# A transformer block's gates: one row of the modulation contracted on VectorE and GpSimd, the other in half-width matvecs

## The chip, the cores and the metric

The kernel runs on one core of a Trainium2 chip. The metric is the time of one execution on the device in microseconds (us), lower being better. Before the change it is 837.8 us, the median of four runs (836.96 to 838.38).

## What is computed

A block of linear attention followed by a gated feed-forward layer, both modulated by a vector c. With S = 2048 rows, D = 1024 and F = 3584, all in bfloat16:

```python
mod = (silu(c) @ w_mod).reshape(6, D)          # w_mod is 1024 x 6144
sa, ca, ga, sb, cb, gb = mod
h = layernorm(x) * (1 + ca) + sa
x = x + ga * linear_attention(h, wqkv, wo)     # 32 heads; q and k through elu + 1
h = layernorm(x) * (1 + cb) + sb
x = x + gb * ((silu(h @ w_gate) * (h @ w_up)) @ w_down)
```

The change concerns ga and gb, two rows of 1024 values, each a product of silu(c) with a 1024 x 1024 slice of w_mod.

## The kernel before

The rows are worked in four chunks of 512 (`NSC`), each of four tiles of 128 rows. TensorE runs one long sequence, kept in program order by `mm` (L98): for each chunk the k and v projections (`k_phase`, `v_phase`), with the k-v product of the chunk before (`kv_phase`) between; then the q projections, the folding of the k-v matrix into wo, and the attention output `wo_tile` (L561) of the first chunk. Then, for each chunk, `gate_up` (L596) and `down` (L622).

`gate_up` walks seven blocks of 512 hidden columns (index `fb`). For a block it loads 1 MB of gate and 1 MB of up weights, both on the synchronous engine's DMA queue. The block has four pairs of accumulators (`fj`), a gate and an up one, eight matmuls of 512 columns each. ScalarE takes the silu of the gate accumulator (L616); VectorE multiplies it with the up accumulator into `gu` (L617), which frees both. The accumulators come from a pool of four PSUM banks. `down` computes eight pieces of 128 x 512 for a chunk, multiplies each by the broadcast row `gb_bc` (L638), adds the residual `x1r` and stores it. Between the pieces the next chunk's `wo_tile`s run: their statistics on VectorE, `rstd` on GpSimd (L211), the store of x1 on GpSimd's DMA queue (L585), and a DMA transpose into `h2T` on the synchronous queue (L588).

In the first `gate_up` a table of callbacks hangs more work behind the last gu product of some blocks (L618 to L620, called at L667). `late_den` makes three den sums on TensorE after block 0, and then, after blocks 0, 2 and 4, broadcasts the reciprocals of the denominators to `rbc` through GpSimd's DMA queue (`den_spread`); after blocks 2, 4 and 6 it multiplies `pq` by them on VectorE (`den_apply`, L427).

The modulation rows are made in three ways. sa and ca come early, in an opening that is interleaved by hand. sb, cb, ga and gb come from `mod_rows` (L364 on): four column blocks of w_mod, 1 MB each (`wml`, loaded by `mod_load`), are multiplied by silu(c), replicated over 32 columns (`sc32`). Four matmuls stand in the four 32-column groups of TensorE at once, one per column block, so all four rows lie in one PSUM bank, `modr`. ScalarE copies the bank to SBUF (`mrow`), GpSimd's queue stores one row of each group to DRAM (`mrow_scratch`), and `mod_spread` reads them back: for k = 0 broadcast over partitions into `ga_bc` and `gb_bc` (L381), for k = 1 as columns sb and cb. The first call stands in chunk 2's k phase with the columns of ga and gb, the second in chunk 3's with those of sb and cb. `ga_bc` is multiplied into wo (L524).

SBUF tiles come from rotating pools; `k8` has 19 buffers of 8 KB a partition for weights and activations, `k2` holds five `x_sb` and four `xn` tiles of 128 x 1024 in bfloat16, `x1p` three f32 tiles `x1`. A scheduler orders each engine's instructions, except where `mm` or `in_order` pins them and where `issue_after` queues work behind a named instruction.

Of the kernel before, what the change touches and what calls it, by code (L numbers as in the profile page):

```python
# [1 line left out]

# [5 lines left out]

# [1 line left out]
ALU = mybir.AluOpType  # L10
BF16 = mybir.dt.bfloat16
F32 = mybir.dt.float32
# [9 lines left out]
def kernel(  # L22
# [13 lines left out]
    nc = tc.nc  # L36
    P = nc.NUM_PARTITIONS
    _, S, D = A_x.shape
# [4 lines left out]
    DC = D // P  # L43
# [3 lines left out]
    NSC = S // SCW  # L47
    STC = SCW // P
    NB = 512
# [16 lines left out]
    wm_v = w_mod.rearrange("(j p) n -> p j n", p=P)  # L66
    c_v = c.rearrange("o (j p) -> (o j) p", p=P)

    const = ctx.enter_context(tc.tile_pool(name="const", bufs=1))
    dram = ctx.enter_context(tc.tile_pool(name="dram", bufs=1, space=DRAM))  # L70
    k8 = ctx.enter_context(tc.tile_pool(name="k8", bufs=19))
    k2 = ctx.enter_context(tc.tile_pool(name="k2", bufs=5))
    x1p = ctx.enter_context(tc.tile_pool(name="x1p", bufs=3))
    ep = ctx.enter_context(tc.tile_pool(name="ep", bufs=3))
    yp = ctx.enter_context(tc.tile_pool(name="yp", bufs=2))
    small = ctx.enter_context(tc.tile_pool(name="small", bufs=4))
# [20 lines left out]
    def mm(out, lhsT, rhs, start, stop):  # L97
        return tc.keep_in_program_order(nc.tensor.matmul(out, lhsT=lhsT, rhs=rhs, start=start, stop=stop))  # L98
# [4 lines left out]
    def big(name, shape):  # L103
        return k8.tile([P] + shape, BF16, name=name, tag="k8")

    def acc_a():
        return pa.tile([P, NB], F32, name="acc", tag="pa")

    def acc_b(name, shape=(NB,), dt=F32):
        return pb.tile([P] + list(shape), dt, name=name, tag="pb")  # L110
# [65 lines left out]
    nc.gpsimd.memset(base[:, :, 1, :], 1.0)  # L176

    scT = const.tile([P, DC], BF16, name="scT")
    sc32 = const.tile([P, DC, 32], BF16, name="sc32")

    sca = const.tile([P, 2, DC], F32, name="sca")
# [4 lines left out]
    sbT = const.tile([P, DC], F32, name="sbT")  # L186
    cb1T = const.tile([P, DC], F32, name="cb1T")
    ga_t = ep.tile([P, NB], F32, name="e")
    ga_bc = ga_t[:].bitcast(BF16)
    gb_bc = const.tile([P, D], BF16, name="gb_bc")  # L190
# [9 lines left out]
    def build_masks():  # L200
        nc.gpsimd.memset(zmask[:], 0.0)
        for h in range(HPC):
            rs = slice(h * DH, (h + 1) * DH)
            for hg in range(HG):
                nc.gpsimd.memset(zmask[rs, hg, HG * h + hg:HG * h + hg + 1], 1.0)
# [52 lines left out]
    def ln1(sc):  # L258
        hTs[sc] = big("hT", [DC, SCW])
        for t in range(STC):  # L260
            ln1_norm(*ln1_stats(sc, t))
# [45 lines left out]
    def k_phase(sc, lo, hi):  # L307
        if lo == 0:
            pks[sc] = big("pk", [STC, D])
        for g in k_groups[lo:hi]:  # L310
            accs = [acc_a()]
            k_mms(sc, [g], accs)
            k_evac(sc, [g], accs)
# [28 lines left out]
    def kv_phase(sc):  # L342
        kvp = acc_b("kvp", (HG, 2, DH))
        for hg in range(HG):
            for t in range(STC):
                for i in range(HPC):
                    mm(kvp[i * DH:(i + 1) * DH, hg, :, :], lhsT=pks[sc][:, t, hg * P + i * DH:hg * P + (i + 1) * DH],
                       rhs=v_ones(vs[sc], t * D + hg * P + i * DH), start=(t == 0), stop=(t == STC - 1))
        kvv = kvp[:].rearrange("p g k e -> p g (k e)")[:, :, 0:DH + 1]
        if sc == 0:  # L350
            nc.vector.tensor_copy(out=kv_acc, in_=kvv)
        else:
            nc.vector.tensor_tensor(out=kv_acc, in0=kv_acc, in1=kvv, op=ALU.add)

    def mod_load(cols):
        blks = []
        for lo in cols:
            t = big("wml", [DC, NB])
            nc.sync.dma_start(out=t[:], in_=wm_v[:, :, lo:lo + NB])
            blks.append(t)  # L360
        return blks

    def mod_rows(blks):
        ps = acc_b("modr")  # L364
        for j in range(DC):
            for g in range(4):
                mm(ps[32 * g:32 * g + 32, :], lhsT=sc32[:, j, :], rhs=blks[g][:, j, :],
                                 start=(j == 0), stop=(j == DC - 1))
        row = small.tile([P, NB], BF16, name="mrow", bufs=1)
        nc.scalar.copy(out=row[:], in_=ps[:])  # L370
        return row

    mrow_dram = dram.tile([2, 4, NB], BF16, name="mrow_scratch")

    def mod_spread(k, row):
        for g in range(4):
            nc.gpsimd.dma_start(out=mrow_dram[k, g:g + 1, :], in_=row[32 * g:32 * g + 1, :])
        if k == 0:
            for dst, g in ((ga_bc, 0), (gb_bc[:], 2)):
                src = mrow_dram[0, g:g + 2, :].rearrange("g n -> (g n)").unsqueeze(0).to_broadcast([P, D])  # L380
                nc.gpsimd.dma_start(out=dst, in_=src)  # L381
        else:
            cols = small.tile([P, 2 * DC], BF16, name="mcol", bufs=1)
            with nc.allow_non_contiguous_dma(reason="2048 elements, once"):
                nc.gpsimd.dma_start(out=cols[:], in_=mrow_dram[1].rearrange("g (i p) -> p (g i)", p=P))
            nc.vector.tensor_copy(out=sbT[:], in_=cols[:, 0:DC])
            nc.vector.tensor_scalar_add(out=cb1T[:], in0=cols[:, DC:2 * DC], scalar1=1.0)

    def modulate_all(hT, scaleT, biasT):
        for cc in range(DC):  # L390
# [51 lines left out]
    with in_order(nc.vector, nc.scalar, nc.gpsimd):  # L442
        mod_ps = acc_b("mod_ps")
        mm(mod_ps[:, A * 64:A * 64 + DC], lhsT=c_sb[:], rhs=ident[0:DC, 0:DC], start=True, stop=True)
        for g in range(4):
            mm(mod_ps[32 * g:32 * g + 32, 0:A * 64], lhsT=ident[:, 0:32], rhs=base_t[:, 0:A * 64],
               start=True, stop=False)
# [39 lines left out]
        k_evac(0, gs8, accs8)  # L487
    with tc.issue_after(last_on[nc.gpsimd.engine]):
        build_masks()

    for sc in range(NSC):
        if sc > 0:
            k_phase(sc, 0, 2)
            kv_phase(sc - 1)
            k_phase(sc, 2, 4)
            if sc >= 2:
                mod_spread(sc - 2, mod_rows(blks))
            k_phase(sc, 4, 8)
            if sc == 1:
                blks = mod_load([2 * D, 2 * D + NB, 5 * D, 5 * D + NB])  # L500
            if sc == 2:
                blks = mod_load([3 * D, 3 * D + NB, 4 * D, 4 * D + NB])
        v_phase(sc)
        if sc + 1 < NSC:
            with tc.issue_after(last_on[nc.vector.engine] if sc == 0 else last_phi[-5].ins):
                ln1(sc + 1)
        if sc == 0:
            q_phase(0, 0, 6)
        if sc + 1 < NSC:
            with tc.issue_after(last_phi[0].ins):  # L510
                modulate_all(hTs[sc + 1], ca1T, saT)
        if sc == 0:
            q_phase(0, 6, 8)
        if sc + 2 < NSC:
            for st in range((sc + 2) * STC, (sc + 3) * STC):
                load_x(st, nc.sync)
        if sc == 2:
            wo = [big("wo", [4, D]) for _ in range(2)]
            for h in range(2):
                for g in range(4):  # L520
                    nc.sync.dma_start(out=wo[h][g * DH:(g + 1) * DH, :, :], in_=wo_v[h, g])
            for cc in range(DC):
                w = wo[cc // 4][:, cc % 4, :]
                nc.vector.tensor_tensor(out=w, in0=w, in1=ga_bc, op=ALU.mult)  # L524
# [5 lines left out]
                            in1=zmask[:], op=ALU.mult)  # L530
# [62 lines left out]
    last_w = {}  # L593
    last_mm = {}

    def gate_up(sc, between=None):  # L596
        guT[sc] = []
        for fb in range(NFB):
            wb = []
            for view in (wg_v, wu_v):  # L600
                w = big("wgu", [DC, FBW])
                last_w[sc] = nc.sync.dma_start(out=w[:], in_=view[:, :, fb * FBW:(fb + 1) * FBW])
                wb.append(w)
            for fj in range(FPB):
                f = fb * FPB + fj
                if f % GPT == 0:
                    guT[sc].append(big("gu", [min(GPT, FC - f), SCW]))
                ps = []
                for w in wb:
                    acc = acc_a()  # L610
                    for cc in range(DC):
                        last_mm[sc] = mm(acc[:], lhsT=w[:, cc, fj * P:(fj + 1) * P], rhs=h2Ts[sc][:, cc, :],
                                              start=(cc == 0), stop=(cc == DC - 1))
                    ps.append(acc)
                sg = ep.tile([P, NB], F32, name="e")
                nc.scalar.activation(out=sg[:], in_=ps[0][:], func=ACT.Silu)  # L616
                gm = nc.vector.tensor_tensor(out=guT[sc][f // GPT][:, f % GPT, :], in0=ps[1][:], in1=sg[:], op=ALU.mult)  # L617
            if between and fb in between:  # L618
                with tc.issue_after(gm.ins):
                    between[fb]()  # L620
# [38 lines left out]
    def late_den(sc, sums=()):  # L659
        for s in sums:  # L660
            den_sum(s)
        if sc > 1:
            den_apply(sc - 1)
        if sc < NSC:
            den_spread(sc)

    gate_up(0, {0: lambda: late_den(1, range(1, NSC)), 2: lambda: late_den(2), 4: lambda: late_den(3),  # L667
                6: lambda: late_den(NSC)})
    wd = []
    for b in range(FC // WDF):  # L670
        w = big("wd", [WDF, D])
# [38 lines left out]
```

## Time and profile before

| | |
|---|---|
| median of four runs | 837.8 us |
| the profiled execution, whole | 836.96 us |
| its span in the profile | 835.1 us |
| busy: VectorE, ScalarE, GpSimd | 308.3, 168.9, 61.4 us |
| read from HBM / written | 108.53 / 12.72 MB |
| first `gate_up` on TensorE | 208.5 to 306.8 us |

The profile records one execution; starts are in us from the beginning of the span. PE is TensorE, PEld its weight loads, DVE VectorE, ACT ScalarE, POOL GpSimd, SP the synchronous engine; L617 is line 617. A row of the timeline gives start, duration, engine, line, operation, the tile written and those read, shapes, the count of merged instructions, and in brackets how long the engine was idle before and what ended it. A matmul's recorded duration spans its whole way through the array, so successive ones overlap; what it costs is the distance to the next start. A DMA row on an engine's queue is its issue; the transfer lands later.

### The profile page before, as it was taken

To read this page: it belongs to the slowest core of one execution; us is meant where nothing else is said; L and a number is where in the kernel's file an instruction comes from. 1 tells how busy PE (TensorE), PEld (TensorE's weight loads), DVE (VectorE), ACT (ScalarE), POOL (GpSimd) and SP (SyncE) were. 2 spreads that over 40 slices of the span, in tenths; PEclk is the share of its full clock that TensorE was granted. 3 is DMA by queue.
4 is the path that set the end of the run, shared out by engine and by line. 5 is a ranking of instruction groups with operands and counts; after the bars stand their busy time and mean duration, and the time that the engine had idled before them with its cause. 6 is when DMAs were issued, how large, how long until landed. Compare 5 with 4: busy or idle time off the path is not lost.

```text
span 835.1 us, 11163 instructions
## 1 busy us (share of the span) xinstructions
PE 823.7 (99%) x4560; PEld 378.6 (45%) x4641; DVE 308.3 (37%) x598; ACT 168.9 (20%) x253; POOL 61.4 (7%) x167
## 2 busy tenths in 40 slices
PE   8999999999999999999999999999999999999998
PEld 3444444444444444444444444444444444444444
DVE  5755643587413325521122344211114431111122
ACT  3445443334211111101111110111110101111000
POOL 2101201111130001100000010000001100000000
PEclk9999999999999999999999999999999999999999
DMA  9793790129987447336434182662504529610011
GB/s 331 287 291 79 243 210 1 30 66 273 364 200 260 151 151 208 120 114 219 146 109 144 44 228 95 224 217 77 175 1 152 164 70 345 225 53 1 18 58 51
DMA packets 126755, 129.33 MB, mean 155 GB/s; under 512 B 34032, under 2 KB 108272, under 8 KB 126192
## 3 DMA queue, kind: packets, MB, share of 16 engines
q1 hardware_dynamic: 122368, 114.97, 44.8%
q0 software_dynamic: 4048, 13.25, 5.3%
q8 instruction: 36, 0.59, 0.3%
q10 hardware_dynamic: 288, 0.40, 0.1%
q14 instruction: 15, 0.12, 0.0%
HBM read 108.53 MB, written 12.72 MB: 145 GB/s over the span
## 4 chain that ended last, share of the span: by engine, by line
PE 96%; DMA 2%; issue 1%; DVE 0%; ACT 0%; ACTq 0%; SPq 0%
PE acc L98 88%; PE a_ps L98 7%; DMA wme<-in_w_mod_dram 1%; DMA wml<-in_w_mod_dram 1%; PE modr L98 0%; PE kvp L98 0%; PE den L98 0%; PE mod_ps L98 0%; DVE wo L548 0%; PE wf L98 0%; DVE pq L291 0%; ACT eb L288 0%; ACTq L125 0%; PE tp L101 0%; SPq L134 0%
## 5 line engine op out<-in xcount | busy, mean ns | idle before, releaser
L98 PE MATMUL acc<-h2T,wgu 128*128 128x512 bf16 x1756 | 385.7, 379 | 1.9
L98 PEld LDWEIGHTS <-wgu 128*128 128x128 bf16 x1792 | 175.3, 98 | 211.3
L98 PE MATMUL acc<-wd,gu 128*128 128x512 bf16 (+2 forms) x908 | 195.2, 372 | 0.9
L617 DVE TENSOR_TENSOR gu<-acc,e 128x512 bf16<-128x512 f32 x112 | 77.5, 692 | 299.3 <-PE acc L98 288.2
L616 ACT ACTIVATE e<-acc 128x512 f32<-128x512 f32 x112 | 67.0, 598 | 374.6 <-PE acc L98 363.2
L98 PEld LDWEIGHTS <-gu 128*128 128x128 bf16 x924 | 89.3, 98 | 104.5
L98 PEld LDWEIGHTS <-hT 128*128 128x128 bf16 x512 | 49.6, 98 | 60.0 <-issue 0.9
L638 DVE TENSOR_TENSOR e<-acc,gb_bc 128x512 f32<-128x512 f32 (+2 forms) x33 | 22.3, 675 | 132.2 <-PE acc L98 125.9
L98 PE MATMUL acc<-wk,hT 128*128 128x512 bf16 x248 | 56.5, 379 | 0.8 <-issue 0.3
L98 PE MATMUL a_ps<-wo,pq 128*128 128x512 bf16 x250 | 56.9, 379 | 0.3
L98 PE MATMUL acc<-hT,wq 128*128 128x512 bf16 x247 | 55.6, 379 | 0.9 <-issue 0.6
L98 PE MATMUL acc<-wv,hT 128*128 128x512 bf16 x251 | 55.6, 379 | 0.3
L288 ACT ACTIVATE eb<-acc 128x512 bf16<-128x512 f32 x64 | 37.9, 596 | 74.4 <-PE acc L98 71.2
L227 ACT ACTIVATE xn<-x,nmr,rstd 128x1024 bf16<-128x1024 f32 x16 | 19.8, 1240 | 126.3 <-POOL nmr L225 126.3
L585 POOL DMA_DIRECT2D x_scratch<-x x16 | 9.7, 608 | 418.2 <-DVE x L578 418.2
L98 PEld LDWEIGHTS <-pq 128*128 128x128 bf16 x256 | 25.0, 98 | 30.2
L98 PEld LDWEIGHTS <-wq 128*128 128x128 bf16 x256 | 24.6, 98 | 29.8 <-issue 0.9
L289 DVE TENSOR_SCALAR eb<-eb 128x512 bf16<-128x512 bf16 x64 | 18.3, 290 | 49.7 <-ACT eb L288 49.6
L578 DVE TENSOR_TENSOR x<-a_ps,x_sb 128x512 f32<-128x512 f32 x32 | 22.1, 691 | 7.9 <-PE a_ps L98 7.1
L211 POOL TENSOR_TENSOR rstd<-veps,neg_half 128x1 f32<-128x1 f32 x32 | 17.9, 560 | 73.6 <-DVE veps L209 71.3
L326 ACT CAST v<-acc 128x512 bf16<-128x512 f32 x32 | 18.4, 583 | 23.1 <-PE acc L98 22.5
L641 DVE TENSOR_TENSOR ob<-e,x1r 128x512 bf16<-128x512 f32 (+2 forms) x33 | 22.3, 675 | 1.0
(76 smaller groups left out, 259.2 us busy)
## 6 DMA issues: line engine op xcount, KB each, us to landing
wgu<-in_B_w_gate_dram SPq DMA_DIRECT2D x28, 1024.0 KB, 7.0
wgu<-in_B_w_up_dram SPq DMA_DIRECT2D x28, 1024.0 KB, 7.9
x_sb<-in_A_x_dram SPq DMA_DIRECT2D x32, 256.0 KB, 6.5
wml<-in_w_mod_dram SPq DMA_DIRECT2D x8, 1024.0 KB, 9.1
x_scratch<-x POOLq DMA_DIRECT2D x16, 512.0 KB, 3.0
x1r<-x_scratch SPq DMA_DIRECT2D x31, 256.0 KB, 2.8
wd<-in_B_w_down_dram SPq DMA_DIRECT2D x7, 1024.0 KB, 6.1
rbc<-rden_scratch POOLq DMA_DIRECT2D x16, 256.0 KB, 5.5
```

The costliest lines, as they stand in the source:

```text
L98: return tc.keep_in_program_order(nc.tensor.matmul(out, lhsT=lhsT, rhs=rhs, start=start, stop=stop))
L211: nc.gpsimd.tensor_tensor(out=rstd[:, 0:n], in0=veps[:, 0:n], in1=neg_half[:].to_broadcast([P, n]), op=ALU.pow)
L227: nc.scalar.activation(out=dst, in_=src, func=ACT.Identity, bias=nmr[:], scale=rstd[:, 0:1])
L288: nc.scalar.activation(out=e[:], in_=acc, func=ACT.Exp)
L289: nc.vector.tensor_scalar(out=e[:], in0=e[:], scalar1=1.0, scalar2=PHI_EPS, op0=ALU.min, op1=ALU.add)
L326: nc.scalar.copy(out=v[:, t * D + nb * NB:t * D + (nb + 1) * NB], in_=acc[:])
L578: nc.vector.tensor_tensor(out=x1[:, ns], in0=a_ps[:], in1=x_t[:, ns], op=ALU.add)
L585: nc.gpsimd.dma_start(out=x1_dram[st * P:(st + 1) * P, :], in_=x1[:])
L616: nc.scalar.activation(out=sg[:], in_=ps[0][:], func=ACT.Silu)
L617: gm = nc.vector.tensor_tensor(out=guT[sc][f // GPT][:, f % GPT, :], in0=ps[1][:], in1=sg[:], op=ALU.mult)
L638: nc.vector.tensor_tensor(out=yt, in0=y_ps, in1=gb_bc[:, ns], op=ALU.mult)
L641: nc.vector.tensor_tensor(out=ob, in0=yt, in1=x1r, op=ALU.add)
```

## The change

The row gb no longer goes through TensorE. `gb_load` reads the 1024 x 1024 slice of w_mod as eight tiles of 128 x 1024, 256 KB each, into five `x_sb` and three `xn` buffers, on the synchronous queue behind the weight loads of the first gate/up's block 1. `gb_sum` multiplies each by its column of silu(c) (`scf`, an f32 copy) and accumulates in f32 in `gb_acc`: one product and four multiply-adds after block 1, three after block 3. Then one GpSimd instruction sums `gb_acc` over the 128 partitions and leaves the total in every partition of `gb_bc`.

The row ga keeps its matmuls. Its 1024 columns now fill all four 32-column groups with 256 columns each (`ga_rows`), from two `wml` blocks instead of four; row stores and broadcast follow with pieces of 256. `mod_spread` keeps only its branch for sb and cb.

```diff
+    scf = const.tile([P, DC], F32, name="scf")
...
+    def gb_load():
+        for j in range(DC):
+            t = k2.tile([P, D], BF16, name="x_sb") if j < 5 else k2.tile([P, D], BF16, name="xn", bufs=4)
+            nc.sync.dma_start(out=t[:], in_=wm_v[:, j, 5 * D:6 * D])
+            gb_rows.append(t)
+
+    def gb_sum(lo, hi):
+        for j in range(lo, hi):
+            t, sc = gb_rows[j], scf[:, j:j + 1]
+            if j == 0:
+                nc.vector.tensor_scalar(out=gb_acc[:], in0=t[:], scalar1=sc, scalar2=None, op0=ALU.mult)
+            else:
+                nc.vector.scalar_tensor_tensor(out=gb_acc[:], in0=t[:], scalar=sc, in1=gb_acc[:], op0=ALU.mult, op1=ALU.add)
+
+    def ga_rows(blks):
+        ps = acc_b("modr")
+        H2 = NB // 2
+        for j in range(DC):
+            for g in range(4):
+                mm(ps[32 * g:32 * g + 32, 0:H2], lhsT=sc32[:, j, :], rhs=blks[g // 2][:, j, (g % 2) * H2:(g % 2 + 1) * H2],
+                   start=(j == 0), stop=(j == DC - 1))
+        row = small.tile([P, NB], BF16, name="mrow", bufs=1)
+        nc.scalar.copy(out=row[:, 0:H2], in_=ps[:, 0:H2])
+        for g in range(4):
+            nc.gpsimd.dma_start(out=mrow_dram[0, g:g + 1, 0:H2], in_=row[32 * g:32 * g + 1, 0:H2])
+        nc.gpsimd.dma_start(out=ga_bc.rearrange("p (g n) -> p g n", g=4),
+                            in_=mrow_dram[0, :, 0:H2].unsqueeze(0).to_broadcast([P, 4, H2]))
...
-        if k == 0:
-            for dst, g in ((ga_bc, 0), (gb_bc[:], 2)):
-                src = mrow_dram[0, g:g + 2, :].rearrange("g n -> (g n)").unsqueeze(0).to_broadcast([P, D])
-                nc.gpsimd.dma_start(out=dst, in_=src)
...
     with tc.issue_after(last_on[nc.gpsimd.engine]):
         build_masks()
+        nc.gpsimd.tensor_copy(out=scf[:], in_=scT[:])
...
-            if sc >= 2:
-                mod_spread(sc - 2, mod_rows(blks))
+            if sc == 2:
+                ga_rows(blks)
+            if sc == 3:
+                mod_spread(1, mod_rows(blks))
             k_phase(sc, 4, 8)
             if sc == 1:
-                blks = mod_load([2 * D, 2 * D + NB, 5 * D, 5 * D + NB])
+                blks = mod_load([2 * D, 2 * D + NB])
...
-    gate_up(0, {0: lambda: late_den(1, range(1, NSC)), 2: lambda: late_den(2), 4: lambda: late_den(3),
-                6: lambda: late_den(NSC)})
+    def gb_first():
+        with tc.issue_after(last_w[0].ins):
+            gb_load()
+        gb_sum(0, 5)
+
+    def gb_last():
+        gb_sum(5, DC)
+        nc.gpsimd.partition_all_reduce(gb_bc[:], gb_acc[:], P, bass_isa.ReduceOp.add)
+
+    gb_acc = x1p.tile([P, D], F32, name="x1")
+    gate_up(0, {0: lambda: late_den(1, range(1, NSC)), 1: gb_first, 2: lambda: late_den(2), 3: gb_last,
+                4: lambda: late_den(3), 6: lambda: late_den(NSC)})
```

In the instruction streams of the changed kernel, VectorE's order in block 2 is one product and two multiply-adds, a gu product, two multiply-adds, the next gu product; the three of block 3 stand together before the first gu product of block 4. On GpSimd the sum over partitions stands after the first of the last four `rbc` broadcasts and before the other three. One library instruction precedes it, and another stands between the x1 store and `rstd` of the next chunk's first `wo_tile`. The eight row loads stand on the synchronous queue between the weights of block 1 and those of block 2.

More of the change, by code (lines that the diff above doesn't have):

```diff
@@ L4 @@
 import concourse.tile as tile
-from concourse import bass_utils, mybir
+from concourse import bass_isa, bass_utils, mybir
 from concourse._compat import with_exitstack
@@ L353, in kv_phase @@
             nc.vector.tensor_tensor(out=kv_acc, in0=kv_acc, in1=kvv, op=ALU.add)
+    def gb_load():
[23 more added lines that the diff above has]
+                            in_=mrow_dram[0, :, 0:H2].unsqueeze(0).to_broadcast([P, 4, H2]))
+    gb_rows = []
     def mod_load(cols):
@@ L377, in mod_spread @@
             nc.gpsimd.dma_start(out=mrow_dram[k, g:g + 1, :], in_=row[32 * g:32 * g + 1, :])
-        if k == 0:
-            for dst, g in ((ga_bc, 0), (gb_bc[:], 2)):
-                src = mrow_dram[0, g:g + 2, :].rearrange("g n -> (g n)").unsqueeze(0).to_broadcast([P, D])
-                nc.gpsimd.dma_start(out=dst, in_=src)
[L382 to L387, printed above, removed]
+        cols = small.tile([P, 2 * DC], BF16, name="mcol", bufs=1)
+        with nc.allow_non_contiguous_dma(reason="2048 elements, once"):
+            nc.gpsimd.dma_start(out=cols[:], in_=mrow_dram[1].rearrange("g (i p) -> p (g i)", p=P))
+        nc.vector.tensor_copy(out=sbT[:], in_=cols[:, 0:DC])
+        nc.vector.tensor_scalar_add(out=cb1T[:], in0=cols[:, DC:2 * DC], scalar1=1.0)
     def modulate_all(hT, scaleT, biasT):
```

## The prediction

> **What bounds the kernel now.** I read the page from the top: busy times, then the chain that ended last, then the timelines of TensorE, VectorE and GpSimd over the stretches that the change touches. From the page:
>
> ```profile
> PE 823.7 (99%) x4560; PEld 378.6 (45%) x4641; DVE 308.3 (37%) x598; ACT 168.9 (20%) x253; POOL 61.4 (7%) x167
> ...
> PE 96%; DMA 2%; issue 1%; DVE 0%; ACT 0%; ACTq 0%; SPq 0%
> ```
>
> TensorE works for 823.7 of 835.1 us and the chain is 96% TensorE. Time can go only where TensorE's own work shrinks; it can come wherever another engine makes it wait. Of the 11.4 us idle, 3.05 lie in the first 30 us and 4.2 after 600 us, where nothing changes. The clock row is 9 in all 40 slices and the windows give a granted clock of 1.00, so no clock is to be won. TensorE's timeline around the two mod-row blocks, and through the first gate/up stage:
>
> ```profile
> 95.12 1.91 PE L98 MATMUL modr<-wml,sc 128*32 128x512 bf16 x32
> 96.96 7.08 PE L98 MATMUL acc<-wk,hT 128*128 128x512 bf16 x31
> ...
> 208.50 13.98 PE L98 MATMUL acc<-h2T,wgu 128*128 128x512 bf16 x63
> 222.41 1.52 PE L98 MATMUL den<-pq,Zden 128*32 128x128 bf16 x96
> 223.86 83.05 PE L98 MATMUL acc<-h2T,wgu 128*128 128x512 bf16 x376
> 306.75 6.21 PE L98 MATMUL acc<-wd,gu 128*128 128x512 bf16 x27
> ```
>
> The first column is the start. The first mod-row block holds TensorE from 95.12 until the next projection starts at 96.96, 1.84 us. The stage runs without a gap from 208.50 to 306.75: seven blocks of four pairs, a pair 3.455 us (the spacing of VectorE's products below), and 1.45 us of den sums. VectorE and GpSimd in that stage:
>
> ```profile
> 265.59 0.69 DVE L617 TENSOR_TENSOR gu<-acc,e 128x512 bf16<-128x512 f32 x1 [2.76 <-PE acc L98]
> ...
> 279.40 0.69 DVE L617 TENSOR_TENSOR gu<-acc,e 128x512 bf16<-128x512 f32 x1 [2.76 <-PE acc L98]
> 280.01 2.48 DVE L427 TENSOR_TENSOR pq<-pq,rbc 128x1024 bf16<-128x1024 bf16 x4
> 282.85 0.69 DVE L617 TENSOR_TENSOR gu<-acc,e 128x512 bf16<-128x512 f32 x1 [0.36 <-PE acc L98]
> ...
> 241.67 1.94 POOL L419 DMA_DIRECT2D rbc<-rden_scratch  x4 [1.29 <-PE acc L98]
> 317.44 0.57 POOL L585 DMA_DIRECT2D x_scratch<-x  x1 [73.83 <-DVE x L578]
> 318.53 0.56 POOL L211 TENSOR_TENSOR rstd<-veps,neg_half 128x1 f32<-128x1 f32 x1 [0.52 <-DVE veps L209]
> ```
>
> VectorE is idle 2.76 us of each 3.455. GpSimd is idle from 243.6 to 317.4.
>
> **Removed from TensorE.** The first block's 32 matmuls go from 512 to 256 columns. They run four at a time: 1.84 us / 8 groups = 230 ns a group. The den sums have the same shape with 128 columns: 1.45 us / 24 = 60.4 ns. Between the two a column costs (230 − 60.4)/384 = 0.44 ns, so a 256-column group is 60.4 + 128 × 0.44 = 117 ns, eight are 0.94 us, and **0.90 us** goes. The 0.16 us that the next projection waited for a wml load at 91.7 may go too; I don't count it. The second block stays 1.84.
>
> **Early transfers.** Two 1 MB wml loads leave the synchronous queue at 49 to 56 us, and the gate's broadcast leaves GpSimd's (0.56 us of issue at 103.0). The ga broadcast now moves pieces of 256 elements. Nothing waits for less than it did: the wo product that reads ga waited for TensorE (3.1 us), not for it. The scheduler reorders some statistics and normalisations at 97 to 107 us; the hT tile made there is modulated by 115.0 and used at 117.69. Those 2.7 us hide a slip; a larger one would be TensorE's.
>
> **The eight row loads, 2 MB.** They stand on the synchronous queue behind the second block's weights (issued 199.74 and 200.98), ahead of the third's. From 217 to 231 us the DMA moves 340 GB/s, full, so everything behind them slips by 2.1 MB / 340 GB/s = 6.2 us. The third block's up weights were issued at 208.99 with at most 13.6 us to landing: 222.6, now 228.8, against a first use at 208.50 + 2 × 13.82 + 1.45 = 237.6. The fourth's 214.79 + 13.6 + 6.2 = 234.6 against 251.4. The first rbc set, issued from 232.4 to 234.3, landed within 10.9 us; with the slip 251.4 against 252.38. All hidden, the last by 1 us plus VectorE's slack below. The rows have landed before their first read at 238.65. Their buffers, x_sb and xn, were last read before 198, and x_sb is wanted again at 255.35, after the five sums.
>
> **VectorE: one product and seven multiply-adds, 128x1024 in f32.** Nearest is the all-SBUF group ob<-e,x1r: 292 ns at 128 columns, 691 at 512, thus 1.04 ns a column and 1.22 us at 1024. A bf16 product of 1024 (xn<-x_sb, 0.546 us) is the lower end for the first; I take 1.22 for all, 9.8 us. Three come behind the second block's last product at 238.65, then a gu product, then two; three more behind the fourth block. Three take 3.67 us where 2.76 were idle, so a gu product comes 0.9 to 1.0 us late. What waits for it is the accumulator of the up matmuls two pairs on: with four accumulators these begin 3.455 + 1.73 = 5.2 us after the pair's end, the product needs 0.69 and started 0.1 after that end, so it may come **4.3 us** late at no cost. Hidden, with sums of up to 2.3 us each (3 × 2.3 − 2.7 = 4.2).
>
> **The sum over partitions on GpSimd.** It waits for the last three sums: 266.28 + 3.7 = 270.0. No row shows this operation. The lower end is one pass as in the 128x128 select of identity (0.283 us; less some 0.1 for the start, 1.4 ns a column): 1.5 us. The upper end is the Trainium skill, "GPSIMD Engine Reference", section 3.2: 247.7 us for a reduction along partitions at [128, 2048], an estimated 124 at 1024. That is another instruction, and one that doesn't look worth using; the same page's section 3.1 has 1.8 to 2.6 cycles an element at 1.2 GHz, and a sum that folds, passes along the cores, returns and writes is some four such passes. I take **9 us**, nearer the row: 270 to 279. Queued behind it are three of the last four rbc broadcasts; at 279 + 1.5 + 10.9 = 291.4 they are in time for 307.63. Its own reader, the first gate product, stands at 313.0.
>
> **The rule that speaks against it.** The skill's "SBUF — State Buffer", "Who interferes with whom": a VectorE instruction with two SBUF inputs and a GpSimd instruction that reads SBUF exclude each other for the whole instruction. The gu products read PSUM and one SBUF tile and are free of it; the four pq products at 280.01 are not. The trace can't show this lock, GpSimd being idle there. By the row they start at 280.01 anyway. By the rule they start when GpSimd ends, and the gu product behind them may slip to 287.1, so they may start at 284.6: with 9 us nothing is lost, and from 14.6 us each further us costs TensorE one.
>
> **Two library loads on GpSimd.** The first follows the first of those rbc broadcasts, near 242, and has 28 us of idle time over it. The second stands between the x1 store at 317.44 and rstd at 318.53. Neither is in the trace; nothing below, and some 6 us each above by "GPSIMD Engine Reference", section 2.1. I take 6: the first transposed h2T tile goes from 320.75 to about 327, and gate weights queued behind it slip likewise. The second stage starts at 306.75 + 8 × 6.05 + 4 × 3.45 = 369. Hidden; a load over some 25 us would hold result stores and reach TensorE.
>
> **Sum.** The profiled execution took 836.96 us (span 835.1 and 1.86 around it): minus 0.90 gives 836.1. It was the lowest of four runs; the median, 837.8, lies 0.84 higher, so I forecast **836.9**. A measurement of this kernel can tell 0.2%, 1.7 us, from no change; this is half of that.
>
> **Rivals.**
> 1. *GpSimd holds the shared port over the pq products* (slower). Place 280.01, price T − 14.6 us for a sum that takes T, decisive from T = 14.6. For: the rule, and no row for T. Against: the idle window and the estimate. T = 20 gives 836.9 + 5.4 = 842.3; 30 gives 852.3; the page's 124 about 946.
> 2. *The added traffic lands late*, at the first pq products (252.38), where only a few us stand over the estimate and the DMA is full. Three us past the cover give 840. Against: the maxima of landing were used.
> 3. *More goes than the matmuls*: fewer early transfers close gaps too. TensorE idles 2.1 us between 30 and 208 us; half of it gives 835.9. Against: the waits view puts nearly all of these gaps to issue, 0.2 us to the DMA.
> 4. *The halving yields nothing*, because weight loads or issue set the pace of the small matmuls: 837.8. Against: the den row's 60 ns for four.
>
> **How the numbers follow.** The forecast, with its own range 835.9 to 838.3: 0.60. Rival 1: 0.14; rival 2: 0.10; rival 3: 0.10; rival 4: 0.06. Faster, below 836.1: rival 3's better part and the forecast's lower edge, 0.15. Same: most of the forecast and rival 4, 0.62. Slower, above 839.5: rivals 1 and 2, nearly, 0.23. The range reaches up to T = 20 with rival 1, 842.5, and down to 835.6.
>
> **What would show it.** Right: modr's 32 matmuls in about 1 us; TensorE without a gap from 208 to 306; gu products at most 1 us late; the sum over by 280. Wrong: pq products at 280 that wait for GpSimd; a wgu or rbc landing as the reason of a TensorE wait; h2T transposes still open near 369.

## The result, and the profile after

The changed kernel takes **836.36 us** (median of 36 runs, 835.89 to 837.12) against 837.78 for the kernel before (56 runs, 836.96 to 838.86): a ratio of 0.9983, 95% interval 0.9979 to 0.9988. That is 1.4 us less, just under what 0.2% would be. The forecast was 836.9.

The two profiled executions hide part of it: 834.8 us of span after, 835.1 before. Their openings differ: TensorE's first k projection starts at 14.96 us in the one and at 15.64 in the other. In the other seven kernels below that share the changed kernel's opening it starts between 14.92 and 15.85, so this much varies from run to run, and from there on differences are what counts. TensorE's timeline after, with start and duration first:

```profile
95.52 1.06 PE L98 MATMUL modr<-wml,sc 128*32 128x256 bf16 x32
96.51 7.08 PE L98 MATMUL acc<-wk,hT 128*128 128x512 bf16 x31
...
208.04 13.98 PE L98 MATMUL acc<-h2T,wgu 128*128 128x512 bf16 x63
221.95 1.52 PE L98 MATMUL den<-pq,Zden 128*32 128x128 bf16 x96
223.41 83.05 PE L98 MATMUL acc<-h2T,wgu 128*128 128x512 bf16 x376
306.30 6.21 PE L98 MATMUL acc<-wd,gu 128*128 128x512 bf16 x27
```

The mod-row block holds TensorE for 0.99 us (95.52 to 96.51) where it was 1.84: **0.85 us**. The first gate/up stage has the same rows, to the hundredth, as before (13.98, 1.52, 83.05): nothing that was added stops it once. From the block's end to the stage's end both kernels need 209.79 us (96.96 to 306.75, and 96.51 to 306.30). VectorE's timeline where the products of the gb row stand:

```profile
237.50 0.69 DVE L646 TENSOR_TENSOR gu<-acc,e 128x512 bf16<-128x512 f32 x1 [2.76 <-PE acc L98]
238.11 0.74 DVE L366 TENSOR_SCALAR x<-x_sb,scf 128x1024 f32<-128x1024 bf16 x1
238.89 2.60 DVE L368 SCALAR_TENSOR_TENSOR x<-x_sb,scf,x 128x1024 f32<-128x1024 bf16 x2
241.41 0.68 DVE L646 TENSOR_TENSOR gu<-acc,e 128x512 bf16<-128x512 f32 x1
242.01 2.59 DVE L368 SCALAR_TENSOR_TENSOR x<-x_sb,scf,x 128x1024 f32<-128x1024 bf16 x2
...
265.74 3.92 DVE L368 SCALAR_TENSOR_TENSOR x<-xn,scf,x 128x1024 f32<-128x1024 bf16 x3
269.57 0.68 DVE L646 TENSOR_TENSOR gu<-acc,e 128x512 bf16<-128x512 f32 x1
...
279.55 2.49 DVE L453 TENSOR_TENSOR pq<-pq,rbc 128x1024 bf16<-128x1024 bf16 x4
```

The gu product due at 237.50 + 3.455 = 240.95 comes at 241.41; the one after block 3, due at 268.59, at 269.57, 1 us late. The pq products at 279.55 take their usual 2.49 us. And GpSimd's timeline:

```profile
269.79 6.13 POOL L703 PARTITION_ALL_REDUCE gb_bc<-x  x1 [23.91 <-DVE x L368]
275.81 1.70 POOL L445 DMA_DIRECT2D rbc<-rden_scratch  x3
316.98 0.58 POOL L614 DMA_DIRECT2D x_scratch<-x  x1 [39.48 <-DVE x L607]
324.58 0.59 POOL L212 TENSOR_TENSOR rstd<-veps,neg_half 128x1 f32<-128x1 f32 x1 [7.01 <-DVE x L607]
```

The sum over partitions takes 6.13 us and is over at 275.9, 3.6 us before the pq products. The `rstd` whose input was ready at 317.84 (VectorE's veps, 317.69 + 0.15) starts at 324.58: 6.7 us for the library load. No wait of TensorE follows from it.

One thing remains. In both profiles, count from the k-v product of chunk 0 to the next v projection: 62.37 to 73.05 before, 63.06 to 73.43 after, 10.68 against 10.37 us for the same 47 matmuls. The row of TensorE there, first before, then after:

```profile
62.37 2.55 PE L98 MATMUL acc<-wk,hT 128*128 128x512 bf16 x10
65.07 8.14 PE L98 MATMUL acc<-wk,hT 128*128 128x512 bf16 x37 [0.15 <-issue]
```

```profile
63.06 10.53 PE L98 MATMUL acc<-wk,hT 128*128 128x512 bf16 x47
```

The pause before 65.07 is gone. It has no cause that the profile names. The view by windows, of before and then of after, with the DMA's share and its GB/s last, shows what else is different around it:

```profile
57.00:62.00 5.00, 5.00 (x119) 2.55 (x118) 4.26 (x13) 1.79 (x3) 0.00 (x0) 1.00 1.09 349
```

```profile
57.00:62.00 5.00, 4.95 (x35) 2.16 (x37) 4.90 (x14) 1.62 (x3) 0.00 (x0) 1.00 0.07 21
```

Before, the four wml loads keep the DMA full up to this point; after, the two that are left have landed. So there were two candidates for the 1.4 us: 0.85 from the matmuls, and some 0.3 from the two loads that no longer come early. (The 0.15 in brackets is less than the loss of 0.31, because successive matmuls overlap by 0.16 us in their records: 379 ns long, 216 ns apart.)

### The profile page after: what moved, and what is told of

Its sections match the earlier page's. It is cut to its first block, busy times and chain, and to the rows that moved or that the text cites. A ratio compares the mean times of both kernels' runs of the same rounds, so it can differ in the third digit from the quotient of the medians.

```text
span 834.8 us, 11191 instructions
## 1 busy us (share of the span) xinstructions
PE 823.5 (99%) x4560; PEld 378.6 (45%) x4641; DVE 317.3 (38%) x606; ACT 168.6 (20%) x253; POOL 67.7 (8%) x168
## 4 chain that ended last, share of the span: by engine, by line
PE 97%; DMA 2%; issue 1%; DVE 0%; ACT 0%; ACTq 0%; SPq 0%
PE acc L98 89%; PE a_ps L98 7%; DMA wme<-in_w_mod_dram 2%; PE kvp L98 1%; PE modr L98 0%; PE den L98 0%; PE mod_ps L98 0%; DVE wo L577 0%; PE wf L98 0%; DVE pq L292 0%; ACT eb L289 0%; ACTq L125 0%; PE tp L101 0%; SPq L134 0%; DVE eb L290 0%
```

## Experiments

All times are medians. The kernel before ran beside each on the same chip: at 837.72 beside the two loads taken away, the gb row left out, the banks in turn and the other gate's row, at 837.76 beside the other four. Ratios are against it.

### The matmuls' width alone

```diff
-                mm(ps[32 * g:32 * g + 32, 0:H2], lhsT=sc32[:, j, :], rhs=blks[g // 2][:, j, (g % 2) * H2:(g % 2 + 1) * H2],
+                mm(ps[32 * g:32 * g + 32, :], lhsT=sc32[:, j, :], rhs=blks[g // 2][:, j, :],
...
```

> The changed kernel, with the first mod-row block back at 512 columns a matmul (each half row is computed twice, one copy is used); the loads stay at two blocks. Theory A (the gain is TensorE's matmul time, 0.85 us, plus about 0.3 us of TensorE gaps near 65 us that the two missing loads leave out): the block takes 1.84 us again, the time is 0.85 us over the changed kernel, 837.2, some 0.5 under the kernel before. Rival B (all 1.4 us come from the shorter matmuls and what they shift): 837.8. Rival C (the matmul width is worth nothing, the loads all): 836.4.

Measured: 837.18 us, ratio 0.9994 (0.9986 to 1.0003); the block takes 1.84 us again (95.71 to 97.55):

```profile
95.71 1.91 PE L98 MATMUL modr<-wml,sc 128*32 128x512 bf16 x32
97.55 7.08 PE L98 MATMUL acc<-wk,hT 128*128 128x512 bf16 x31
```

That is 0.82 over the changed kernel, as theory A has it. Rival C (836.4) falls. Rival B (837.8) is 0.6 off the median, but the interval still holds it; what speaks against it is the trace, here and in the next experiment. What is left below the kernel before, 0.58 by the medians, is not the width.

### The two loads, put back and taken away

Put back into the changed kernel, unused:

```diff
-                blks = mod_load([2 * D, 2 * D + NB])
+                blks = mod_load([2 * D, 2 * D + NB, 5 * D, 5 * D + NB])
```

> The changed kernel, with the two 1 MB blocks of the gb row loaded again near 50 us, and not used. Theory A: TensorE has its gap of 0.15 us near 65 us again and the projection from 63 to 73 us takes 10.7 us, not 10.4; 836.7. Rival B: 836.4, no gap. Rival C: 837.8.

Measured: 836.54 us, ratio 0.9985 (0.9979 to 0.9992). TensorE's timeline of this run:

```profile
62.56 2.55 PE L98 MATMUL acc<-wk,hT 128*128 128x512 bf16 x10
65.44 8.15 PE L98 MATMUL acc<-wk,hT 128*128 128x512 bf16 x37 [0.34 <-issue]
```

The pause is back at the same instruction, behind the tenth matmul; the time lies between theory A and rival B. And taken away from the kernel before:

```diff
-                blks = mod_load([2 * D, 2 * D + NB, 5 * D, 5 * D + NB])
+                blks = mod_load([2 * D, 2 * D + NB]) * 2
```

> The kernel before, with only two 1 MB blocks loaded for the first mod rows; the four 512-column matmul rows read these two twice, so the gb row is a copy of ga's. Theory A: the pause of TensorE near 65 us and the slower stretch behind it (10.68 us instead of 10.37 from 62.4 to 73) are gone; the time falls by 0.2 to 0.3 us, to 837.5. If the loads are worth nothing: 837.8. If they are the whole of what the wide-matmul experiment kept (837.18): 837.2.

Measured: 837.30 us, ratio 0.9995 (0.9987 to 1.0004); TensorE goes from 62.83 to 73.20 without a pause, 10.37 us:

```profile
62.83 10.53 PE L98 MATMUL acc<-wk,hT 128*128 128x512 bf16 x47
```

The pause thus follows the loads in all ten kernels traced: there with four loads (before, and the changed kernel with two put back), absent in the eight with two. In the trace it costs 0.31 us (10.68 − 10.37), and 0.50 in the second case (62.56 to 73.43, 10.87). In the times it is 0.42 here and 0.18 there, and neither is clear of the noise: the first interval reaches 1, the second overlaps the changed kernel's.

The traces add up better than the times. From the first k projection to the end of the first gate/up, TensorE needs 291.79 us before, 291.48 with the two loads taken away, 291.49 with the width alone put back, 291.13 with the two loads put back, and 290.66 in the changed kernel. That is 0.83 for the width, 0.31 to 0.47 for the loads, nothing (0.01) for the move of the gb row to VectorE, and 1.13 in all. The remaining 0.3 of the 1.4 us lies outside that stretch or between one execution and another, and stays open.

What the pause waits for can be read from the DMA packets. Besides the data, queue 8 moves instructions, 36 packets of 16 KB in every one of the traces. The DMA view of 60 to 66 us counts one of them before, then two after:

```profile
q8 instruction: 1, 0.02, 1.1%
```

```profile
q8 instruction: 2, 0.03, 2.2%
```

By the packets' own records, the third packet of the queue starts at 62.64 us before and at 63.04 with the two loads put back, and between 60.02 and 60.76 in the eight kernels without the pause. It takes 0.9 to 1.2 us. In the two kernels that pause, TensorE goes on 1.35 and 1.27 us after it has landed; in the eight others it landed at least 3.7 us before TensorE came to that instruction. So the reading that fits all ten is that the packet stands behind the wml loads and TensorE waits for it. That these packets are TensorE's is inferred from this match; nothing in the trace names the engine that they are for.

### The gb row left out

```diff
-            gb_load()
-        gb_sum(0, 5)
+        nc.vector.memset(gb_bc[:], 1.0)
...
-        gb_sum(5, DC)
-        nc.gpsimd.partition_all_reduce(gb_bc[:], gb_acc[:], P, bass_isa.ReduceOp.add)
...
```

> The changed kernel without the gb row: no row loads, no sums on VectorE, no sum over partitions and no library loads; gb is taken as 1. Theory A (all of that is covered): 836.36, as the changed kernel, within 0.2. If something of it costs time behind the trace's back: below 836.1.

Measured: 836.61 us, ratio 0.9987 (0.9981 to 0.9994), 0.25 above the changed kernel, whose interval it overlaps. Without 2 MB of loads, 9.8 us of VectorE work, the sum and two library loads the kernel is no faster, and TensorE's stretch from the first k projection to the end of the first gate/up is 290.63 us against 290.66. All of it is covered. The `rstd` that waited 6.7 us behind its input in the changed kernel starts here at 317.32 after 0.52 us of idle time that VectorE ended, so that wait goes with the sum and its library.

### How much VectorE's cover holds

The prediction rested on a gu product being free to come 4.3 us late. All eight products in one stretch overdraw that:

```diff
-        gb_sum(0, 5)
+        gb_sum(0, DC)
+        hold.append(gb_last_sum[0])
...
-        gb_sum(5, DC)
...
-                gm = nc.vector.tensor_tensor(...)
+                with tc.issue_after(hold[0].ins) if hold and sc == 0 and fb == 2 else ExitStack():
+                    gm = nc.vector.tensor_tensor(...)
```

> The changed kernel, with all eight products of the gb row in one stretch on VectorE after block 1, before any gu product of block 2. They take 0.74 + 7 x 1.30 = 9.8 us from 238.1, to 248.0; the next gu product is due at 240.9 and comes 7.1 us late. If the cover is the 4.3 us of the prediction, TensorE stops for 2.8 us and the time is 839.2. If the cover is larger than 7 us (the accumulators are not what binds): 836.4. If VectorE has no cover at all: 843.5.

Measured: 836.32 us, ratio 0.9984 (0.9977 to 0.9990). The gu product came at 247.63, 7.1 us late, and TensorE did not stop. So the cover seemed larger than 7 us. The program as built suggests why: in it the third pair's up accumulator lies in the bank of the second pair's gate accumulator, which ScalarE frees early, and not in that of the first pair's up accumulator. In the changed kernel as built the four banks simply take turns. The second experiment forces that turn:

```diff
-    pa = ctx.enter_context(tc.tile_pool(name="pa", bufs=4, space=PSUM))
+    pa = ctx.enter_context(tc.tile_pool(name="pa", bufs=1, space=PSUM))
...
-        return pa.tile([P, NB], F32, name="acc", tag="pa")
+        turn[0] += 1
+        return pa.tile([P, NB], F32, name="acc", tag=f"pa{turn[0] % 4}")
```

> All eight products in one stretch, as before in e5_sums_in_a_row, but the accumulators now take the four PSUM banks in turn; instruction order is that of e5_sums_in_a_row on every engine. There the late gu product cost nothing, and its build had given the third pair's up accumulator the bank of the second pair's gate accumulator. Theory A (the cover is 4.3 us with the banks in turn, as in the changed kernel, and the allocator stretched it): the gu product comes 6.7 to 7.1 us late, TensorE waits 2.4 to 2.8 us before the third pair's up matmuls, 838.8 to 839.2. Rival (the cover was never 4.3): no wait, 836.3.

Measured: 839.28 us, ratio 1.0023 (1.0016 to 1.0030). TensorE's and VectorE's timelines of this run:

```profile
223.16 22.62 PE L99 MATMUL acc<-h2T,wgu 128*128 128x512 bf16 x101
248.51 60.59 PE L99 MATMUL acc<-h2T,wgu 128*128 128x512 bf16 x275 [2.72 <-DVE gu L650]
```

```profile
237.26 0.69 DVE L650 TENSOR_TENSOR gu<-acc,e 128x512 bf16<-128x512 f32 x1 [2.76 <-PE acc L99]
...
247.77 1.28 DVE L650 TENSOR_TENSOR gu<-acc,e 128x512 bf16<-128x512 f32 x2
```

The gu product was due at 237.26 + 3.455 = 240.72 and came 7.05 us late. The brackets show 2.72 us of idle time, but the distance between starts shows more: from 223.16 to the first down matmul at 308.94 are 85.78 us, and the changed kernel needs 82.89 (223.41 to 306.30), so TensorE lost 2.89. That agrees with the time, 2.9 over the changed kernel. The cover is 7.05 − 2.89 = **4.16 us** where the banks take turns. The same lateness costs 2.9 us or nothing, by the placement of the accumulators; no other wait of TensorE is new in this run.

### The lock on VectorE's second input

```diff
-        nc.gpsimd.partition_all_reduce(gb_bc[:], gb_acc[:], P, bass_isa.ReduceOp.add)
+        for _ in range(4):
+            nc.gpsimd.partition_all_reduce(gb_bc[:], gb_acc[:], P, bass_isa.ReduceOp.add)
```

> The changed kernel, with the sum over partitions made four times over in a row on GpSimd. Each takes 6.1 us, so they fill 269.8 to about 295 us, over the four pq products at 279.5. Theory L (a GpSimd instruction that reads SBUF locks out a VectorE instruction with two SBUF inputs until it ends): the first pq product starts only near 282, the next ones each wait for a sum too, to some 295 to 300 us, and TensorE, which can spare 4.3 us, loses 8 to 13 us: 844 to 849. Rival N (no lock that can be seen): the pq products start at 279.5 and take 2.5 us, the time is 836.4. A middle: the products are stretched by sharing, up to 4 us, without a loss of time.

Measured: 836.34 us, ratio 0.9983 (0.9977 to 0.9990). GpSimd's timeline, then the view of the tile rbc in this run (shortest, median and longest duration in ns, first and last start):

```profile
276.74 6.07 POOL L704 PARTITION_ALL_REDUCE gb_bc<-x  x1
282.68 0.51 POOL L445 DMA_DIRECT2D rbc<-rden_scratch  x1
283.22 6.33 POOL L704 PARTITION_ALL_REDUCE gb_bc<-x  x1
```

```profile
L453 DVE TENSOR_TENSOR pq<-pq,rbc x4: 679/680/2051, 279.7 to 282.9; 128x1024 bf16<-128x1024 bf16 x4
```

Neither theory L nor its rival. One of the four products is held, the first: it starts at 279.72 and takes 2.05 us instead of 0.68, so its work began at 281.09, which is 4.35 us after the sum began at 276.74 and 1.7 us before it ended. The other three run freely, all of them started before the next sum, at 283.22. The gu product at 279.11, which has one input in SBUF and one in PSUM, takes its usual 0.69 within the first 4.4 us of the same sum. The two experiments on VectorE's cover give the same from other offsets, since their pq products also fell into a sum. In the first of them, with the sum on GpSimd and the tile view:

```profile
250.04 6.13 POOL L705 PARTITION_ALL_REDUCE gb_bc<-x  x1 [6.30 <-DVE gu L648]
```

```profile
L454 DVE TENSOR_TENSOR pq<-pq,rbc x4: 678/680/3576, 251.5 to 256.2; 128x1024 bf16<-128x1024 bf16 x4
```

251.54 + 3.58 − 0.68 = 254.44, 4.40 us after the sum's start; in the second (sum at 251.03, first product at 254.56, 1.54 long) 4.39. So there is a lock, but it lasts the first 4.4 us of this instruction, not its 6.1. Why it ends there the records don't show.

### The other gate's row in the same way

Since the stage's covers were not used up, the ga row went the same way: its products on VectorE in the gaps of chunk 2's and 3's v projections, the sum over partitions behind them.

```diff
-            if sc == 2:
-                ga_rows(blks)
...
-                blks = mod_load([2 * D, 2 * D + NB])
+                blks = load_w(wm_v, 2 * D, "wml")
...
+        if sc == 3:
+            with tc.issue_after(last_phi[0].ins):
+                ga_sum(6, DC)
+            par = nc.gpsimd.partition_all_reduce(ga_bc, ga_acc[0][:], P, bass_isa.ReduceOp.add)
...
```

`ga_sum` is `gb_sum` over the two wml tiles; products 0 to 3 follow chunk 2's phi work, 4 and 5 the modulation of chunk 3's hT; the wo product moves behind the sum. A one-element power behind the sum brings GpSimd's library back while it is idle.

> The changed kernel, with the ga row made in the same way: six of its eight products on VectorE beside the third chunk's v projection, two beside the fourth's, then a sum over partitions near 138 us, and the wo product behind it. TensorE's first mod-row block (0.99 us) is gone. Theory A (TensorE's time is all that counts): 835.4. If the wo product ends too late for VectorE's phi work behind it (it is due at 149.7 and the product ends near 149.5), some tenths to 2 us come back: 835.6 to 837.4.

Measured: **835.23 us** (835.18 to 835.67), ratio 0.9973 (0.9963 to 0.9983): 1.1 below the changed kernel and 2.5 below the kernel before, the fastest of all. VectorE's and GpSimd's timelines:

```profile
137.54 2.59 DVE L376 SCALAR_TENSOR_TENSOR x<-wml,scf,x 128x1024 f32<-128x1024 bf16 x2
146.44 4.90 DVE L537 TENSOR_TENSOR wo<-wo,e 128x1024 bf16<-128x1024 bf16 x8 [6.30 <-POOL e L530]
151.27 0.29 DVE L290 TENSOR_SCALAR eb<-eb 128x512 bf16<-128x512 bf16 x1
```

```profile
140.28 6.13 POOL L530 PARTITION_ALL_REDUCE e<-x  x1 [7.54 <-DVE x L376]
146.28 0.18 POOL L533 MEMSET one<- 128x1 f32 x1
153.52 0.59 POOL L534 TENSOR_TENSOR one<-one,neg_half 128x1 f32<-128x1 f32 x1 [7.06 <-issue]
```

The wo product ends at 151.3, after the phi work behind it was due; VectorE catches up before TensorE needs it. A pause, again named "issue", now stands at 94.55 on TensorE:

```profile
91.95 2.32 PE L98 MATMUL acc<-wk,hT 128*128 128x512 bf16 x10 [0.16 <-issue]
94.55 8.16 PE L98 MATMUL acc<-wk,hT 128*128 128x512 bf16 x37 [0.28 <-issue]
```

The DMA is full there with the second block's loads (share 1.05 from 80 to 92 us), but it is just as full in the changed kernel (1.05), which does not pause. What differs is the instruction packet: here it lands at 93.16, and TensorE goes on 1.39 us later, at 94.55; in the changed kernel it lands at 92.79, and TensorE passes the same instruction at 94.34 without a pause. Up to the end of the first gate/up TensorE gains 0.66 us on the changed kernel (290.00 against 290.66). The rest of the 1.1 isn't in this trace, whose execution, at 835.67, was the slowest of the eight. In this version only the rows that are needed as columns are left on TensorE.

## Why the prediction was right, point by point

The sign, the bound and the mechanism were right: a gain that stays under 0.2%, taken from TensorE's matmuls, with everything added covered. The size was 0.9 and is 1.4; the stated range, 2.4 us wide, was wide enough to hold the difference. The forecast named the larger part of the gain, the 0.83 to 0.85 of the width, and put the other part at nothing.

- **The matmuls.** 0.94 us forecast for the half-width block, 0.99 measured; the gain 0.90 against 0.85 in the trace and 0.82 in the times. The interpolation between the 512-column and 128-column rows gave 117 ns for a group of four; it is 124.
- **Early transfers: the term that was mis-sized.** The sum put them at nothing; rival 3 put them at 1 us or so and had the mechanism nearly right. The missing loads take away a pause that costs 0.3 to 0.5 us in the traces. The prediction read TensorE's waits, found "issue" beside nearly all of the gaps, and concluded that transfers had no part in them. The experiments show that one of these gaps depends on transfers. The one it did put to a load, 0.16 us at 91.7, stayed (92.17, now under "issue"; 0.16 in all ten traces), so that releaser was a coincidence.
- **The row loads.** A slip of 6.2 us behind them was forecast. The third block's gate weights were issued at 214.78 instead of 203.92, its up weights at 215.47 instead of 208.99 and the fourth's up weights at 219.78 instead of 214.79, so 10.9, 6.5 and 5.0 us; all were in time, and so was the first rbc set, which I had given only 1 us and VectorE's cover.
- **VectorE.** 1.22 us a product forecast, 1.30 for the multiply-adds, 0.74 for the first; 9.8 us in all, as forecast. Lateness 1 us, as forecast. The cover was given as 4.3; its sum as written, 5.2 − 0.69 − 0.1, is 4.4, and the measured one is 4.16 with the banks in turn. A lateness of 1 us is far inside either, so the slip cost nothing.
- **The sum over partitions.** 9 us taken between 1.5 and 124; it is 6.13. The skill's figure for the reduction at [128, 2048] in "GPSIMD Engine Reference", halved, is twenty times too long for this instruction; the four passes that the 9 us came from were nearer.
- **Rival 1** had a real lock with the wrong length. It was priced at one us for each beyond 14.6, with GpSimd holding to the end. In the changed kernel the sum is over before the pq products, so it never came into play there. The skill's "SBUF — State Buffer", "Who interferes with whom", calls it an exclusive lock, and the page has it held for the whole instruction; the measured hold is 4.4 of 6.1 us, in three runs. Whether a second sum queued behind could hold the rest wasn't tested, since they had all started before it.
- **Library loads.** 6 us taken, 6.7 and 7.1 measured, hidden.
- **Rivals 2 and 4** didn't happen: no wait on a landing in the stage, and the halved matmuls did take about half.

## What to carry to other kernels

Where one engine works 99% of the span, a gain is what you take off that engine, and the question for all that is moved elsewhere is how late it may come there; that lateness can be worked out from the buffers between the two engines, here to within 0.3 us, but only for a known placement of the buffers. A short reduction over partitions of weights by a vector needn't be a matmul: products on an engine with gaps and one sum across partitions cost TensorE nothing here, twice. And gaps named "issue" in a profile are not free of the memory traffic around them: look at the DMA's share at that moment, and at when the instruction queue's packets landed, before calling them fixed.

## What the runs showed that I had not expected

The sum over partitions of 128 x 1024 f32 takes 6.1 us every time, in eleven records from 6.06 to 6.33, and holds a VectorE instruction with two SBUF inputs for its first 4.4 us only. It seems to work the other way too: at one place of the last version an `rstd` of one element, 0.55 us otherwise, took 1.58 us and the small product after it 0.95 instead of 0.27, at 107.5 to 110.2, while VectorE ran three multiply-adds with two SBUF inputs from 107.42 to 111.35.

TensorE's pauses named "issue" that come and go, at 65.07, 65.44 and 94.55 us in three of the ten traces, all end 1.27 to 1.39 us after a packet of the instruction queue has landed, and at neither of the two places does TensorE go on sooner than that in any trace. A full DMA near a pause is thus not the whole of it: what counts is whether the packet has landed some 1.3 us before TensorE comes to the instruction. No experiment delayed such a packet by itself.
